# One-hot selection and the sum of output halves moved to GpSimd and DMA in a clustered attention and two-layer-pair kernel

## The chip, the cores and the metric

The kernel runs as one program on one core of a Trainium2 chip. The time is device microseconds of one execution. Lower is better. Five engines work side by side, each through its own instructions in order: TensorE (PE; PEld is its weight load), VectorE (DVE), ScalarE (ACT), GpSimd (POOL), and SyncE (SP), which here issues every transfer. TensorE writes to PSUM; GpSimd works on SBUF alone.

## The reference

Inputs are float32: q, k, v of 2 x 8 x 768 x 64, centroids of 8 x 16 x 64, and the weights of two pairs of layers. First comes attention within clusters; each query and key belongs to the centroid with the greatest cosine, and pairs in different clusters are masked:

```python
q_assign = np.argmax(np.einsum('bhsd,hcd->bhsc', q_n, c_n), axis=-1)
k_assign = np.argmax(np.einsum('bhsd,hcd->bhsc', k_n, c_n), axis=-1)
mask = q_assign[:, :, :, None] == k_assign[:, :, None, :]
scores = scale * np.matmul(q, k.transpose(0, 1, 3, 2))
scores = np.where(mask, scores, -1000000000.0)
scores = scores - np.max(scores, axis=-1, keepdims=True)
attn = np.exp(scores)
attn = attn / (np.sum(attn, axis=-1, keepdims=True) + 1e-09)
attn_out = np.matmul(attn, v)
```

The result, 1536 tokens of 512, goes through `relu(x @ w_in)**2 @ w_out` (512 to 2048 to 512; the float64 weights are read as pairs of 32-bit words), and then through four experts of 512 to 1024 to 512 whose outputs are weighted with `domain_probs` and summed.

## The kernel before, in words

**Numbers.** Matrices are split in two: a rounded float32r "high" part and a "low" part, the difference. A product takes three matmuls in the two layer pairs. In attention the high and low parts are stacked: `vv` holds the high part of v in 64 columns and the low part in the other 64, so one matmul gives two halves of the output that must be added.

**Attention.** There are 16 heads of 6 query blocks of 128 (96 blocks, numbered g or u in the code). For a block, `emit_S` makes the scores (four matmuls of 384 columns, L479; the first two over q and k, the last two over a low part and, in 16 more rows, a one-hot code of the cluster that does the masking), `emit_max` the row maximum on VectorE (L488), `emit_exp` the exponential on ScalarE (L499), `emit_T` six transposes on TensorE (L512) with the rounding copy on ScalarE (L517, `pth`) and the difference on VectorE (L518, `ptl`), `emit_PV` the product with `vv` (L526, L528; 12 matmuls for two blocks). `emit_PO` (L533) takes the product of two blocks out of PSUM: ScalarE copies one half to `tmp` (L542), VectorE adds the other (L544) into `xs`.

**What prepares a head.** Pairs of heads are loaded together. Four transpose slots per pair (`trans_slot`) leave `kqf` by ScalarE; GpSimd rounds it by adding a broadcast tile of zeros (L361) and subtracts (L363) into `nkh`, `nkl`, `nqh`, `nql`. `stack` (L367) copies these by DMA into the stacked tiles k1, q0, q1, k2, q2. `assign_slot` multiplies with the centroids (12 matmuls, L384); `onehot_ops` (L396) finds the greatest cosine and turns it to a one-hot code in seven VectorE operations (L420 to L427), the last two writing `oh`; ties go to the first centroid by the weights `wgt`. Two `onehot_slot`s transpose the code by three tiles each (L440), ScalarE copies it to `ohm` (L445), and two transfers (L448) put it into rows 64 to 79 of q2 and k2.

**What ends a pair of heads.** `norm_slots` makes the reciprocal of the row sums (f1), transposes it (f2), spreads it over rows with matmuls and multiplies (f3, L584), rounds (L596) and subtracts (L598) on GpSimd into `xh` and `xl`, the input of the layers.

**What sets the order.** Engines run in the order in which the code issues. `ORDER` (L24) lists the steps of an even and of an odd block: S, M and E are scores, maximum and exponential of later blocks, T, H and L the transposes and their two exits, P0 and P1 the product, O its exit, X1 and X2 two places for a slot and Y1, Y2 for its exit, R loads, stacks and the split of v, C one operation of the one-hot chain from the list `dq`, K one step of weight conversion from the list `cq` (even blocks from the eighth on). `AT` (L30) says how many blocks before a head its slots come, `START` (L28) where they come for the first heads. A one-hot slot first issues all that is left in `dq`. ScalarE's and GpSimd's instructions are issued at the slot's exit, so GpSimd's queue holds, in this order for an odd head, the split of v, four splits of k and q, and for an even head the exit of f3.

**Weights.** The first chunk of `w_in` is converted from float64 words during attention (`split64`, five VectorE operations on `cva` for each of four blocks, L153 to L165, issued as three and then two at one K, then a rounding and a subtraction); two loads of 1 MB of `w_out` follow in the same list. The rest is loaded and converted during the layers (`run_plan`), where TensorE works through 144 blocks of `gemm1` (L618 to L620) and `gemm2` (L648).

Of the kernel before, what the change touches and what calls it, by code (L numbers as in the profile page):

```python
# [34 lines left out]
def moe_attention_kernel(  # L35
# [15 lines left out]
    def eng(x):  # L51
        return {"V": nc.vector, "P": nc.gpsimd}[FL[x]]

# [43 lines left out]
    w_t = {}  # L97

# [36 lines left out]
    def split64(ci, part, j, cv):  # L135
# [13 lines left out]
        def f1():  # L149


            a = st["a"] = cv.tile(shp, F32, tag="cva", name="cva")
            nc.vector.tensor_scalar(  # L153
                a.bitcast(I32), high, 0x7FFFFFFF, None, op0=ALU.bitwise_and)
            nc.vector.tensor_scalar(a, a, 2.0 ** -15, None, op0=ALU.max)
            nc.vector.tensor_scalar(
                a.bitcast(I32), a.bitcast(I32), 3, 0x3FFFFFF8,
                op0=ALU.logical_shift_left, op1=ALU.bitwise_and)

        def f2():  # L160
            ai = st["a"].bitcast(I32)
            nc.vector.scalar_tensor_tensor(  # L162
                out=ai, in0=high, scalar=-0x40000000, in1=ai,
                op0=ALU.bitwise_and, op1=ALU.bitwise_or)
            nc.vector.scalar_tensor_tensor(  # L165
                out=ai, in0=low, scalar=29, in1=ai,
                op0=ALU.logical_shift_right, op1=ALU.bitwise_or)
# [6 lines left out]
        return [[f1, f2], [f3]]  # L174
# [23 lines left out]
    with tc.manual_schedule():  # L198
# [77 lines left out]
        vt, stk, kq, ohs, ohm = {}, {}, {}, {}, {}  # L276
        dq = []

        def split_v(i):
# [4 lines left out]
            if FL["vh"] == "A":  # L284
                nc.scalar.copy(hi, a)
            else:
                nc.gpsimd.tensor_tensor(hi, a, zeros.to_broadcast([128, NTT, D]), op=ALU.add)
            eng("vl").tensor_tensor(
                vv[:, :, D - vo:2 * D - vo], a, hi.bitcast(F32), op=ALU.subtract)

        def double(i, nm):
# [3 lines left out]
            for e in range(2):  # L295
                if i == 0:
                    nc.vector.tensor_copy(t[:, :, e], x)
                else:
                    nc.gpsimd.tensor_tensor(
                        t[:, :, e], x, zeros.to_broadcast([128, NTT, D]), op=ALU.add)  # L300
# [9 lines left out]
        def split_direct(i, nm, m):  # L310
# [14 lines left out]
            if nm == "nk":  # L325
# [6 lines left out]
                        lambda: nc.gpsimd.tensor_tensor(  # L332
                            second[top], both[top].bitcast(F32),
                            zeros[top].to_broadcast([D, 2, HALF]), op=ALU.add))
# [6 lines left out]
        def trans_slot(j, nm, half):  # L341

            def f():
# [52 lines left out]
        def onehot_ops(i, A):  # L396
# [7 lines left out]
            def p1():  # L404
                nc.gpsimd.tensor_tensor(A, A, mx.to_broadcast(shp), op=ALU.subtract)
                nc.gpsimd.tensor_scalar(A, A, 0.0, None, op0=ALU.is_ge)
                nc.gpsimd.tensor_tensor(A, A, wgt.to_broadcast(shp), op=ALU.mult)

            def p2():
                nc.gpsimd.tensor_tensor(A, A, mx2.to_broadcast(shp), op=ALU.subtract)  # L410
                nc.gpsimd.tensor_scalar(
# [547 lines left out]
```

## Time and profile before

| | |
|---|---|
| three runs | 1105.01, 1106.34, 1107.47 us; median 1106.34 |
| the profiled execution | 1102.88 us, its span 1100.8 us |
| TensorE (PE) busy | 1066.0 us, 97% of the span |
| VectorE (DVE) busy | 546.6 us, 50% |
| ScalarE (ACT) busy | 441.5 us, 40% |
| GpSimd (POOL) busy | 297.1 us, 27% |
| mean granted clock of TensorE | 0.992 |

The span runs from the first to the last instruction; what lies around it is the difference to the execution's time. Busy is the union of an engine's instructions. Attention fills the first 305 us or so, the layers the rest. In rows in order of time, the first number is the start in us from the span's start, the second the duration, "xN" says that N instructions of one kind stand in the row, and a bracket at the end gives idle time of the engine before it and what ended it. In rows of groups, what stands behind the bar is the group's busy us, the mean ns of one, and the idle us before them.

### The profile page before, as it was taken

What the parts mean: (1) busy time and instruction counts of PE and PEld (TensorE: products, weight loads), DVE (VectorE), ACT (ScalarE), POOL (GpSimd) and SP (SyncE); (2) the same over time, 40 slices, a digit from 0 to 9 for tenths busy, and PEclk for the clock granted to TensorE, in tenths of its full rate; (3) what the DMA queues carried; (4) which work ended last, traced back from release to release, by engine and by line L of the source; (5) the groups of instructions that cost most, each with busy time, mean ns of one, the idle gap of its engine ahead of it and who ended that gap; (6) DMA issues with size and microseconds to landing.
All of it is one profiled execution on the core that took longest, in us unless ns stands there. A gap on an engine that the chain in (4) does not pass through costs nothing.

```text
span 1100.8 us, 14190 instructions
## 1 busy us (share of the span) xinstructions
PE 1066.0 (97%) x5502; PEld 903.7 (82%) x5502; DVE 546.6 (50%) x950; ACT 441.5 (40%) x894; POOL 297.1 (27%) x300
## 2 busy tenths in 40 slices
PE   7887989999999999999999999999999999999998
PEld 7786879898877888888888888888888888888886
DVE  8799979999978884741012322222222223222322
ACT  6576778888855553434432121111212112121110
POOL 3346436544212222224544021110202112020000
PEclk9899999999999999999999999999999999999999
DMA  5564385645112331220111111020111101000012
GB/s 150 131 149 110 81 229 118 143 113 114 27 34 84 112 115 39 77 77 0 41 37 39 39 39 39 1 77 1 39 39 39 39 1 45 32 1 1 1 39 76
DMA packets 51810, 70.60 MB, mean 64 GB/s; under 512 B 25664, under 2 KB 28224, under 8 KB 51744
## 3 DMA queue, kind: packets, MB, share of 16 engines
q1 hardware_dynamic: 51744, 69.70, 22.9%
q8 instruction: 43, 0.70, 0.3%
q14 instruction: 23, 0.19, 0.1%
HBM read 43.05 MB, written 3.15 MB: 42 GB/s over the span
## 4 chain that ended last, share of the span: by engine, by line
PE 84%; DVE 11%; ACT 2%; DMA 1%; issue 1%; POOL 1%; SPq 0%; POOLq 0%; DVEq 0%
PE o L648 34%; PE h L620 11%; PE h L618 11%; PE h L619 11%; PE t L512 4%; PE s L479 4%; DVE ptl L518 2%; PE po L526 2%; PE po L528 2%; PE m L384 1%; DVE nb L488 1%; DVE cva L162 1%; DVE cva L165 1%; DMA k<-nkh 1%; PE m L577 1%
## 5 line engine op out<-in xcount | busy, mean ns | idle before, releaser
L632 DVE SCALAR_TENSOR_TENSOR hl<-h,hh 128x512 fp32r<-128x512 f32 x96 | 66.4, 692 | 393.4 <-ACT hh L631 393.4
L631 ACT ACTIVATE hh<-h 128x512 fp32r<-128x512 f32 x96 | 57.4, 598 | 429.0 <-PE h L620 429.0
L618 PE MATMUL h<-xh,w0h 128*128 128x512 f32 x560 | 217.8, 389 | 0.0
L619 PE MATMUL h<-xl,w0h 128*128 128x512 f32 x560 | 217.8, 389 | 0.0
L620 PE MATMUL h<-xh,w0l 128*128 128x512 f32 x560 | 217.8, 389 | 0.0
L648 PE MATMUL o<-w1h,hh 128*128 128x512 f32 x384 | 149.4, 389 | 0.0
L648 PE MATMUL o<-w1l,hh 128*128 128x512 f32 x384 | 149.4, 389 | 0.0
L648 PE MATMUL o<-w1h,hl 128*128 128x512 f32 x384 | 149.4, 389 | 0.0
L618 PEld LDWEIGHTS h<-xh,w0h 128*128 128x128 f32 x560 | 105.3, 188 | 21.8
L620 PEld LDWEIGHTS h<-xh,w0l 128*128 128x128 f32 x560 | 105.1, 188 | 21.9
L619 PEld LDWEIGHTS h<-xl,w0h 128*128 128x128 f32 x560 | 105.1, 188 | 21.7
L629 POOL TENSOR_TENSOR hl<-r,hh 128x512 fp32r<-128x512 f32 x48 | 63.1, 1314 | 184.3 <-ACT hh L628 127.5
L518 DVE TENSOR_TENSOR ptl<-t,pth 128x384 fp32r<-128x384 f32 x192 | 100.2, 548 | 14.9 <-ACT pth L517 13.9
L183 POOL TENSOR_TENSOR w0l<-raw,w0h 128x512 fp32r<-128x512 f32 x32 | 41.3, 1291 | 236.7 <-ACT w0h L182 236.7
L512 PE MATMUL t<-identf,p 128*128 128x128 f32 x576 | 93.3, 287 | 12.2 <-DVE ptl L518 11.2
L488 DVE TENSOR_REDUCE nb<-s 128x1 f32<-128x768 f32 x96 | 90.9, 947 | 10.2 <-PE s L479 9.5
L517 ACT CAST pth<-t 128x384 fp32r<-128x384 f32 x192 | 84.4, 479 | 28.4 <-PE t L512 26.4
L499 ACT ACTIVATE p<-s,nb 128x768 f32<-128x768 f32 x96 | 86.8, 904 | 10.3 <-DVE nb L488 9.7
L479 PE MATMUL s<-k,q 80*128 80x384 f32 (+1 forms) x384 | 88.7, 354 | 0.2 <-DVE q L321 0.2
L512 PEld LDWEIGHTS t<-identf,p 128*128 128x128 f32 x576 | 65.6, 144 | 27.1 <-DVE ptl L518 24.2
L648 PEld LDWEIGHTS o<-w1l,hh 128*128 128x128 f32 x384 | 72.1, 188 | 15.0
L648 PEld LDWEIGHTS o<-w1h,hl 128*128 128x128 f32 x384 | 72.1, 188 | 15.0
(142 smaller groups left out, 1662.3 us busy)
## 6 DMA issues: line engine op xcount, KB each, us to landing
raw<-in_moe_w_dram SPq DMA_DIRECT2D x16, 1024.0 KB, 5.1
raw<-in_moe_w_in_dram SPq DMA_DIRECT2D x8, 1024.0 KB, 5.3
raw<-in_moe_w_out_dram SPq DMA_DIRECT2D x8, 1024.0 KB, 4.9
q<-nqh SPq DMA_DIRECT2D x42, 192.0 KB, 3.0
k<-nkh SPq DMA_DIRECT2D x28, 192.0 KB, 3.9
q<-nql SPq DMA_DIRECT2D x28, 192.0 KB, 3.8
nv<-in_v_dram SPq DMA_DIRECT2D x16, 192.0 KB, 4.3
out_dram<-acc SPq DMA_DIRECT2D x12, 256.0 KB, 2.1
```

The costliest lines, as they stand in the source:

```text
L479: nc.tensor.matmul(s[:, j, 0:HALF], stk[i, nq][:, t * 128:(t + 1) * 128], stk[i, nk][:, j * HALF:(j + 1) * HALF], start=first, stop=not first)
L488: nc.vector.tensor_reduce(out=nb, in_=s_ps[u][:, :, 0:HALF], axis=AX.XY, op=ALU.max, negate=True)
L499: nc.scalar.activation(p, s_ps.pop(u)[:, :, 0:HALF], AF.Exp, bias=nb_t.pop(u), accum_out=sums_t[hp][:, i % 2, t:t + 1])
L512: nc.tensor.transpose(tp[:, j], p_sb[u][:, half, j * 128:(j + 1) * 128], identf)
L517: return (lambda: nc.scalar.copy(dh, tp), lambda: nc.vector.tensor_tensor(dl, tp, dh.bitcast(F32), op=ALU.subtract))
L518: lambda: nc.vector.tensor_tensor(dl, tp, dh.bitcast(F32), op=ALU.subtract))
L618: nc.tensor.matmul(ps, wh[:, kt, ms], xh[tb][:, kt], start=(kt == 0), stop=False)
L619: nc.tensor.matmul(ps, wh[:, kt, ms], xl[tb][:, kt], start=False, stop=False)
L620: nc.tensor.matmul(ps, wl[:, kt, ms], xh[tb][:, kt], start=False, stop=(kt == KD - 1))
L629: nc.gpsimd.tensor_tensor(hl, r, hh.bitcast(F32), op=ALU.subtract)
L632: nc.vector.scalar_tensor_tensor(out=hl, in0=ps, scalar=0.0, in1=hh.bitcast(F32), op0=ALU.max, op1=ALU.subtract)
L648: nc.tensor.matmul(o_t[n], a, b, start=(ft == 0 and z == 0), stop=(ft == NF - 1 and z == 2))
```

## The change

From the third head on, the one-hot chain between the two maxima runs on GpSimd: three operations behind the first maximum (a subtraction, a multiplication by 2^126 in two steps, an addition), four list places left empty, the second maximum on VectorE, then four operations. The comparisons become arithmetic with minimum and maximum, and the query's code is 0 and -1 where it was 1 and 0. Heads 0 and 1 keep VectorE's chain. The one-hot code is transposed two tiles at a time, in one slot a head in place of two, and goes to q2 and k2 in four transfers in place of two.

`emit_PO` copies the whole product (128 partitions) by ScalarE into `xs` or `xo`; when a head is done, transfers move the halves so that high and low parts lie in the same partitions of `xs` and `xm`, and one GpSimd addition per pair of heads (at f2's exit) sums them. The last pair keeps the addition on VectorE.

GpSimd's rounding copies multiply by 1.0 twice (`round_pool`) in place of adding zeros. `kqf` has three buffers in place of two. The five VectorE steps of `split64` are issued one at each K, and the two 1 MB loads of `w_out` become eight of 256 KB, each in a K of its own; the list is 32 entries long in place of 14.

```diff
-START = {'t': [1, 3, 3, 3], 'stack1': 6, 'stack': 7, 'head': [[1, 2, 3], [7, 8, 8]]}
-FL = {"chain": "V", "po": "V", "xh": "P", "xm": "P", "xl": "P", "kh": "P", "kl": "P", "vh": "P", "vl": "P"}
-AT = {"gap": 3, "stack1": -11, "stack": -9, "assign": -9, "oh0": -5, "oh1": -4, "splitv": -3,
+START = {'t': [1, 3, 3, 3], 'stack1': 6, 'stack': 7, 'head': [[1, 2], [7, 8]]}
+AT = {"gap": 4, "stack1": -11, "stack": -9, "assign": -9, "oh": -4, "splitv": -3,
       "t0": -15, "t1": -14, "t2": -13, "t3": -13, "conv": 8}
...
+    def round_pool(dst, src):
+
+        nc.gpsimd.tensor_scalar(dst, src, 1.0, 1.0, op0=ALU.mult, op1=ALU.mult)
...
+    def load_piece(half, n):
+
+        if n == 0:
+            raw_t[0, 1, half] = rawp.tile([128, 2048], F32, tag="raw", name="raw")
+        r = raw_t[0, 1, half].bitcast(I32).rearrange("p (k f) -> p k f", k=2)
+        kk, fs = n // 2, slice((n % 2) * 512, (n % 2) * 512 + 512)
+        nc.sync.dma_start(out=r[:, kk, fs], in_=wo32[:, half * 2 + kk, fs])
...
         def f1():
-
-
             a = st["a"] = cv.tile(shp, F32, tag="cva", name="cva")
+            st["i"] = a.bitcast(I32)
+            nc.vector.tensor_scalar(st["i"], high, 0x7FFFFFFF, None, op0=ALU.bitwise_and)
+
+        def f2():
+            nc.vector.tensor_scalar(st["a"], st["a"], 2.0 ** -15, None, op0=ALU.max)
+
+        def f4():
             nc.vector.tensor_scalar(
-                a.bitcast(I32), high, 0x7FFFFFFF, None, op0=ALU.bitwise_and)
-            nc.vector.tensor_scalar(a, a, 2.0 ** -15, None, op0=ALU.max)
-            nc.vector.tensor_scalar(
...
-        def f2():
-            ai = st["a"].bitcast(I32)
+        def f5():
             nc.vector.scalar_tensor_tensor(
-                out=ai, in0=high, scalar=-0x40000000, in1=ai,
+                out=st["i"], in0=high, scalar=-0x40000000, in1=st["i"],
                 op0=ALU.bitwise_and, op1=ALU.bitwise_or)
+
...
-        return [[f1, f2], [f3]]
+        return [[f1, f2, f4, f5, f6], [f3]]
...
-            if FL["vh"] == "A":
-                nc.scalar.copy(hi, a)
-            else:
-                nc.gpsimd.tensor_tensor(hi, a, zeros.to_broadcast([128, NTT, D]), op=ALU.add)
-            eng("vl").tensor_tensor(
+            round_pool(hi, a)
+            nc.gpsimd.tensor_tensor(
                 vv[:, :, D - vo:2 * D - vo], a, hi.bitcast(F32), op=ALU.subtract)
 
...
-                    x = kq_p.tile([128, HALF], F32, tag="kqf", name="kqf", bufs=2)
+                    x = kq_p.tile([128, HALF], F32, tag="kqf", name="kqf", bufs=3)
                     nc.scalar.activation(x, m, AF.Copy, scale=mul)
-                    if FL["kh"] == "A":
-                        nc.scalar.copy(hi, x)
-                    else:
-                        nc.gpsimd.tensor_tensor(
-                            hi, x, zeros[:, 0].to_broadcast([128, HALF]), op=ALU.add)
-                    eng("kl").tensor_tensor(lo, x, hi.bitcast(F32), op=ALU.subtract)
+                    round_pool(hi, x)
+                    nc.gpsimd.tensor_tensor(lo, x, hi.bitcast(F32), op=ALU.subtract)
...
+            if i > 1:
+
+                P = nc.gpsimd
+
+                def p1():
+                    P.tensor_tensor(A, A, mx.to_broadcast(shp), op=ALU.subtract)
+                    P.tensor_scalar(A, A, 2.0 ** 63, 2.0 ** 63, op0=ALU.mult, op1=ALU.mult)
+                    P.tensor_tensor(A, A, wgt.to_broadcast(shp), op=ALU.add)
+
+                def p2():
+                    P.tensor_tensor(A, A, mx2.to_broadcast(shp), op=ALU.subtract)
+                    P.tensor_scalar(oh[:, :, 0], A[:, NTT:2 * NTT], 0.0, -1.0,
+                                    op0=ALU.min, op1=ALU.max)
+                    P.tensor_scalar(off, A[:, 0:NTT], 0.0, -1.0, op0=ALU.min, op1=ALU.max)
+                    P.tensor_scalar(oh[:, :, 1], off, 1.0, -NEG, op0=ALU.add, op1=ALU.mult)
+
                 return [lambda: V.reduce_max(out=mx, in_=A, axis=AX.X), p1] + [
                     lambda: None] * AT["gap"] + [
                     lambda: V.reduce_max(out=mx2, in_=A, axis=AX.X), p2]
...
+        def onehot_slot(i):
...
+                om = as_p.tile([4 * C, HALF], F32R, tag="ohm", name="ohm")
+                m = ps_m.tile([4 * C, HALF], F32R, tag="m", name="m")
+                for a in range(QT):
                     nc.tensor.transpose(
-                        m[:, t * 128:(t + 1) * 128],
-                        ohs[i][:, half * QT + t].rearrange("p s c -> p (s c)"), identr)
+                        m[:, a * 128:(a + 1) * 128],
+                        ohs[i][:, 2 * a:2 * a + 2].rearrange("p t s c -> p (t s c)"), identr)
 
                 def evac():
-                    nc.scalar.copy(ohm[i][:, half * HALF:(half + 1) * HALF], m.bitcast(F32))
-                    if half == 1:
-                        for nm, r in (("q2", 0), ("k2", C)):
+                    nc.scalar.copy(om, m.bitcast(F32))
+                    for s, nm in enumerate(("q2", "k2")):
+                        for e in range(2):
+                            r = (2 * e + s) * C
                             nc.sync.dma_start(
-                                out=stk[i, nm][D:D + C].bitcast(F32),
-                                in_=ohm[i][r:r + C].bitcast(F32))
+                                out=stk[i, nm][D:D + C].bitcast(F32).rearrange(
+                                    "c (a e n) -> c a e n", a=QT, e=2)[:, :, e],
+                                in_=om[r:r + C].bitcast(F32).rearrange("c (a n) -> c a n", a=QT))
...
-        def emit_PO(pr, last=False):
...
+            po = po_t.pop(pr)
+            cs = slice(jj * 256, (jj + 1) * 256)
+            if e == 0 and jj == 0:
                 xs_t[hp] = xs_p.tile([128, S], F32, tag="xs", name="xs")
-            po = po_t.pop(pr)
-            a, z = D * (i % 2), D * (1 - i % 2)
-            tmp = xs_p.tile([128, 256], F32, tag="tmp", name="tmp")
-            xs = xs_t[hp][a:a + D, jj * 256:(jj + 1) * 256]
-            nc.scalar.copy(tmp[a:a + D], po[z:z + D])
-            if last or FL["po"] == "V":
-                nc.vector.tensor_tensor(xs, po[a:a + D], tmp[a:a + D], op=ALU.add)
-            else:
-                nc.scalar.copy(xs, po[a:a + D])
-                nc.gpsimd.tensor_tensor(xs, xs, tmp[a:a + D], op=ALU.add)
+            if hp == NH // 2 - 1:
+                a, z = D * e, D * (1 - e)
+                tmp = xs_p.tile([128, 256], F32, tag="tmp", name="tmp", bufs=1)
+                nc.scalar.copy(tmp[a:a + D], po[z:z + D])
+                nc.vector.tensor_tensor(xs_t[hp][a:a + D, cs], po[a:a + D], tmp[a:a + D], op=ALU.add)
+                return
+            if e == 1 and jj == 0:
+                xo_t[hp] = xs_p.tile([128, S], F32, tag="xo", name="xo", bufs=1)
+            nc.scalar.copy((xo_t if e else xs_t)[hp][:, cs], po)
+            if jj == NTT // 2 - 1:
+                top, low = slice(0, D), slice(D, 2 * D)
+                if e == 0:
+                    xm_t[hp] = xs_p.tile([128, S], F32, tag="xm", name="xm", bufs=1)
+                    nc.sync.dma_start(out=xm_t[hp][top], in_=xs_t[hp][low])
+                else:
+                    xo = xo_t.pop(hp)
+                    nc.sync.dma_start(out=xs_t[hp][low], in_=xo[low])
+                    nc.sync.dma_start(out=xm_t[hp][low], in_=xo[top])
...
                 def evac():
                     rt = st["rt"] = xs_p.tile([NTT * 4, 128], F32R, tag="rt", name="rt")
                     nc.scalar.copy(rt, m.bitcast(F32))
+                    if hp in xm_t:
+                        xm = xm_t.pop(hp)
+                        nc.gpsimd.tensor_tensor(xs_t[hp], xs_t[hp], xm, op=ALU.add)
                 return evac
...
-                        if last or FL["xh"] == "A":
+                        if last:
                             nc.scalar.copy(hi, xn)
                         else:
-                            nc.gpsimd.tensor_tensor(
-                                hi, xn, zeros[:, 0].to_broadcast([128, n]), op=ALU.add)
-                        (nc.vector if last else eng("xl")).tensor_tensor(
+                            round_pool(hi, xn)
+                        (nc.vector if last else nc.gpsimd).tensor_tensor(
...
+            for n, x in enumerate(("assign", "oh")):
                 at(slots, START["head"][i - 1][n] if i < 3 else u0 + AT[x],
-                   onehot_slot(i, n - 1) if n else assign_slot(i))
+                   onehot_slot(i) if n else assign_slot(i))
...
         cq = []
         for j in range(NF):
             cq += [f for fs in split64(0, 0, j, cv_p[0]) for f in fs]
-        for n, x in enumerate(w_loads(0)[2:]):
-            cq.append(lambda x=x: load_w(*x))
+        for half in range(2):
+            cq += [lambda half=half, n=n: load_piece(half, n) for n in range(4)]
```

## Rows read from the trace of the kernel before

**Rows 1.** Stretch, length, busy us (instructions) of PE, PEld, DVE, ACT, POOL; clock, DMA, GB/s

```profile
58.70:176.80 118.10, 103.63 (x744) 93.74 (x743) 105.30 (x204) 86.27 (x201) 57.90 (x64) 0.96 0.56 133
176.80:276.50 99.70, 97.77 (x741) 89.11 (x739) 93.86 (x186) 83.26 (x197) 50.75 (x60) 1.00 0.56 130
...
346.00:1094.00 748.00, 745.81 (x3291) 617.46 (x3290) 240.56 (x357) 190.57 (x330) 151.16 (x117) 1.00 0.12 40
```

**Rows 2.** The row maxima (L488) alone, heads 8 to 13

```profile
176.80:276.50 99.70, 33.97 (x36) 1.00 0.56 130
```

**Rows 3.** VectorE in order of time, head 11: start us, duration, instruction

```profile
226.31 0.94 DVE L488 TENSOR_REDUCE nb<-s 128x1 f32<-128x768 f32 x1
227.17 0.34 DVE L421 TENSOR_TENSOR A<-A,mx 128x192 f32<-128x192 f32 x1
227.44 1.01 DVE L518 TENSOR_TENSOR ptl<-t,pth 128x384 fp32r<-128x384 f32 x2
...
228.64 0.94 DVE L488 TENSOR_REDUCE nb<-s 128x1 f32<-128x768 f32 x1
```

**Rows 4.** TensorE in order of time, heads 13 and 14

```profile
271.32 0.86 PE L479 MATMUL s<-k,q 128*128 128x384 f32 x4
...
274.70 0.88 PE L479 MATMUL s<-k,q 128*128 128x384 f32 x4
...
282.27 0.87 PE L479 MATMUL s<-k,q 128*128 128x384 f32 x4
282.97 0.34 PE L440 MATMUL m<-identr,oh 128*32 128x128 f32 x3
283.15 0.88 PE L512 MATMUL t<-identf,p 128*128 128x128 f32 x6
...
284.58 0.86 PE L479 MATMUL s<-k,q 128*128 128x384 f32 x4
```

**Rows 5.** VectorE's writers of `oh` (length, busy, count); L544 (count, busy, mean ns)

```profile
58.70:290.00 231.30, 15.22 (x26) 0.98 0.53 126
...
L544 DVE TENSOR_TENSOR xs<-po,tmp 64x256 f32<-64x256 f32 x48 | 20.1, 419 | 2.0 <-ACT tmp L542 1.3
```

**Rows 6.** One operation's duration ns: min, median, max

```profile
L426 DVE TENSOR_SCALAR oh<-off x16: 189/204/1054, 15.6 to 279.6; 128x96 fp32r<-128x96 f32 x16
```

**Rows 7.** Groups of instructions on GpSimd: xcount, busy us, mean ns

```profile
L629 POOL TENSOR_TENSOR hl<-r,hh 128x512 fp32r<-128x512 f32 x48 | 63.1, 1314 | 184.3 <-ACT hh L628 127.5 <-issue 28.6 <-PE o L648 28.1
...
L584 POOL TENSOR_TENSOR rb<-rb,xs 128x384 f32<-128x384 f32 x14 | 14.2, 1014 | 81.0 <-ACT rb L583 81.0
...
L361 POOL TENSOR_TENSOR nkh<-kqf,zeros 128x384 fp32r<-128x384 f32 x14 | 11.8, 839 | 41.3 <-DMA k<-nkh 19.6 <-ACT kqf L357 19.2 <-ACT p L499 2.4
...
masks.py:199 POOL TENSOR_SCALAR_AFFINE_SELECT identf<-identf 128x128 f32<-128x128 f32 x1 | 0.3, 294 | 0.1
```

**Rows 8.** Instructions on `cva` in attention: length, busy of DVE, ACT, POOL

```profile
6.00:300.00 294.00, 13.38 (x20) 2.53 (x4) 5.11 (x4) 0.97 0.52 125
```

**Rows 9.** All engines in order of time, the stall in head 6

```profile
139.15 1.06 SPq L110 DMA_DIRECT2D raw<-in_moe_w_out_dram  x1
...
144.13 0.83 POOL L361 TENSOR_TENSOR nkh<-kqf,zeros 128x384 fp32r<-128x384 f32 x1 [6.74 <-DMA k<-nkh]
...
146.60 0.90 PE L350 MATMUL m<-identf,nq 128*128 128x128 f32 x3 [4.13 <-ACT kqf L357]
```

**Rows 10.** One-hot transfer on SP, its time to landing, and the matmuls that read it

```profile
238.36 0.59 SPq L448 DMA_DIRECT2D k<-ohm  x1
...
DMA to landing us min/median/max: 2.1/2.1/2.2
...
241.75 0.95 PE L479 MATMUL s<-k,q 128*128 128x384 f32 x4
```

**Rows 11.** Fourth split on GpSimd, and the one-hot transposes behind it

```profile
217.07 1.02 POOL L363 TENSOR_TENSOR nql<-kqf,nqh 128x384 fp32r<-128x384 f32 x1
...
220.32 0.42 PE L440 MATMUL m<-identr,oh 128*32 128x128 f32 x3
```

More of the change, by code (lines that the diff above doesn't have):

```diff
@@ L152, in f1, with f6 @@
             a = st["a"] = cv.tile(shp, F32, tag="cva", name="cva")
+            st["i"] = a.bitcast(I32)
[3 more added lines that the diff above has]
+        def f4():
             nc.vector.tensor_scalar(
[L154 to L157 removed]
+                st["i"], st["i"], 3, 0x3FFFFFF8,
                 op0=ALU.logical_shift_left, op1=ALU.bitwise_and)
[L160 to L161 removed]
+        def f5():
             nc.vector.scalar_tensor_tensor(
[L163 removed]
+                out=st["i"], in0=high, scalar=-0x40000000, in1=st["i"],
                 op0=ALU.bitwise_and, op1=ALU.bitwise_or)
+        def f6():
             nc.vector.scalar_tensor_tensor(
[L166 removed]
+                out=st["i"], in0=low, scalar=29, in1=st["i"],
                 op0=ALU.logical_shift_right, op1=ALU.bitwise_or)
@@ L269, in moe_attention_kernel @@
                 idv[:, :, h, 1:2].to_broadcast([NTT * 4, NTT, D]), op=ALU.add)
-        vt, stk, kq, ohs, ohm = {}, {}, {}, {}, {}
+        vt, stk, kq, ohs = {}, {}, {}, {}
         dq = []
@@ L298, in double @@
                 else:
-                    nc.gpsimd.tensor_tensor(
-                        t[:, :, e], x, zeros.to_broadcast([128, NTT, D]), op=ALU.add)
+                    round_pool(t[:, :, e], x)
         def trans_direct(i, nm):
@@ L331, in split_direct @@
                 return (lambda: lo(both[low], low, hi),
-                        lambda: nc.gpsimd.tensor_tensor(
-                            second[top], both[top].bitcast(F32),
-                            zeros[top].to_broadcast([D, 2, HALF]), op=ALU.add))
+                        lambda: round_pool(second[top], both[top].bitcast(F32)))
             else:
@@ L402, in onehot_ops @@
             V = nc.vector
[L404 to L411, printed above, removed]
-                    oh[:, :, 1], A[:, 0:NTT], 0.0, NEG, op0=ALU.is_lt, op1=ALU.mult)
-                nc.gpsimd.tensor_scalar(oh[:, :, 0], A[:, NTT:2 * NTT], 0.0, None, op0=ALU.is_ge)
-            if FL["chain"] == "P" and i > 0:
+            if i > 1:
[10 more added lines that the diff above has]
+                    P.tensor_scalar(oh[:, :, 1], off, 1.0, -NEG, op0=ALU.add, op1=ALU.mult)
                 return [lambda: V.reduce_max(out=mx, in_=A, axis=AX.X), p1] + [
@@ L430, in onehot_ops @@
             ]
-        def onehot_slot(i, half):
+        def onehot_slot(i):
             def f():
@@ L467, in pair_slots @@
             return [trans_slot(j, nm, half) for nm in ("nk", "nq") for half in range(2)]
-        s_ps, p_sb, nb_t, sums_t, pt_t, po_t, xs_t = {}, {}, {}, {}, {}, {}, {}
+        s_ps, p_sb, nb_t, sums_t, pt_t, po_t, xs_t, xo_t, xm_t = {}, {}, {}, {}, {}, {}, {}, {}, {}
         def emit_S(u):
@@ L583, in evac @@
                     nc.scalar.copy(rb, m)
-                    (nc.vector if last else eng("xm")).tensor_tensor(
+                    (nc.vector if last else nc.gpsimd).tensor_tensor(
                         rb, rb, xs_t[hp][:, half * HALF:(half + 1) * HALF], op=ALU.mult)
@@ L592, in evac @@
                         hi = xh[tb][:, kt, o:o + n]
-                        if last or FL["xh"] == "A":
+                        if last:
                             nc.scalar.copy(hi, xn)
                         else:
-                            nc.gpsimd.tensor_tensor(
-                                hi, xn, zeros[:, 0].to_broadcast([128, n]), op=ALU.add)
-                        (nc.vector if last else eng("xl")).tensor_tensor(
+                            round_pool(hi, xn)
+                        (nc.vector if last else nc.gpsimd).tensor_tensor(
                             xl[tb][:, kt, o:o + n], xn, hi.bitcast(F32), op=ALU.subtract)
@@ L799, in moe_attention_kernel @@
                     at(early, START[x] if i == 2 else u0 + AT[x], lambda i=i, n=n: stack(i, n))
-            for n, x in enumerate(("assign", "oh0", "oh1")):
+            for n, x in enumerate(("assign", "oh")):
                 at(slots, START["head"][i - 1][n] if i < 3 else u0 + AT[x],
-                   onehot_slot(i, n - 1) if n else assign_slot(i))
+                   onehot_slot(i) if n else assign_slot(i))
             at(early, u0 + AT["splitv"], lambda i=i: split_v(i))
@@ L893, in moe_attention_kernel @@
         emit_PV(pr, 1)
-        emit_PO(pr, True)
+        emit_PO(pr)
         whole(f3)
```

10 lines of the change are left out of this document (2 added, 8 removed).

## The prediction

> **What bounds the kernel now.** I read the page first, then busy times by stretch, then two engines in order of time. Behind 346 us TensorE is busy for 745.8 of 748 us and VectorE for a third of it [rows 1]; the change touches nothing there, so only attention can move. There a head is six query blocks, each with one row maximum (L488) on VectorE. Heads 8 to 13 are 36 of these in 99.7 us [rows 1, 2], so 2.77 us a block, 16.62 a head. TensorE shows 97.8 us busy there and VectorE 93.9; ScalarE (83.3) and GpSimd (50.8) have room. The two high numbers don't mean the same. TensorE's rows overlap (four score matmuls are written as 0.87 us and the next group starts 0.70 after them [rows 4]), so its union hides short waits. VectorE in order of time has none to hide: from one maximum to the next, 228.64 - 226.31 = 2.33 us, stand the maximum, two `ptl` subtractions and two operations of the one-hot chain at about 0.27 from start to start, no idle mark before any [rows 3]. Without these two it would be 1.8.
>
> What TensorE needs I take from starts, where little is waited for. A block with one one-hot slot takes 284.58 - 282.27 = 2.31, the slot 283.15 - 282.97 = 0.18 of it, so 2.13 without; a block with an assign slot takes 274.70 - 271.32 = 3.38, so the slot costs 1.25 for 12 matmuls, 0.10 each [rows 4]. The head after the change: 6 x 2.13 + 1.25 + 0.18 + about 9.5 small matmuls (transposes of k and q, normalisation) at 0.10 = 15.2 us. Against 16.62 VectorE sets the pace by a small margin.
>
> Heads 2 to 7, as many blocks, take 118.1 us, and VectorE is busy for 105.3 of it [rows 1]. The same work is there, plus 13.4 us of weight conversion on VectorE (20 operations on `cva` [rows 8]) and one stall: a stack transfer lands late next to a 1 MB weight load, GpSimd waits 6.74 us, TensorE 4.13 [rows 9]. The clock granted over this stretch is 0.96, over heads 8 to 13 it is 1.00 [rows 1].
>
> **The change, part by part.** *VectorE, chain.* The two operations that write `oh` are 15.22 us in 13 heads, 1.17 each [rows 5]; the three before them are about 0.34 each [rows 3]. Together 2.2 us a head. *VectorE, halves.* Three additions (L544) a head at 0.419 go, 1.26 [rows 5]; ScalarE's copy stays, with twice the partitions. VectorE falls from 93.86/6 = 15.6 to 12.2 a head, well under TensorE's 15.2; ScalarE is at 83.26/6 = 13.9 [rows 1]. So TensorE is late next.
>
> *GpSimd.* A two-input operation is 1.01 us at 384 and 1.31 at 512 columns [rows 7], so 0.56 at 192 and 1.91 at 768. No row shows a one-input `tensor_scalar` there. From below it isn't cheaper than the 0.29 us of the 128-column select with three times the columns, from above hardly dearer than the two-stream 1.01; the copy with broadcast zeros takes 0.84 [rows 7]. The nearest row is the select (one read, one write), 0.88 if all of it scaled with columns. I take 0.6 at 384, which with the select's 0.29 makes 0.37 at 192 and 0.26 at 96. First part of the chain: 0.56 + 0.37 + 0.56 = 1.5; second: 0.56 + 3 x 0.26 = 1.3. GpSimd's head: 8.5 now [rows 1], + 2.8, + 1.9/2 for the added sum, - 4 x 0.24 for roundings = 11.3 of 15.6. It has the throughput; the question is what waits for it.
>
> The Trainium skill (GPSIMD Engine Reference, section 4.1 Engine selection) speaks against the move: elementwise work belongs on VectorE, GpSimd being about twice as slow with two inputs and roughly at line rate with one. By its line rate at 1.2 GHz a 384-column rounding would be an estimated 0.4 us with a start, and the sum below would be near 1075.
>
> *New waits.* The second maximum on VectorE waits for GpSimd's first part, two blocks after it was issued: hidden; behind it would stand L488 and L518, and TensorE behind those. The one-hot transposes now wait for the second part on GpSimd. For odd heads it is queued behind four k/q splits: these now end at 217.07 + 1.02 = 218.1, the transposes start at 220.32 [rows 11], 2.2 us later. Of this go 1.2 (the one-hot transfers are four instead of two, 0.59 each on SP [rows 10], and the k/q stack transfers that release the splits are queued behind them on SP), 1.2 (five blocks, each 0.23 shorter), 1.3 (second part itself); four cheaper roundings give 1.0 back: 0.5 us late. And the last one-hot transfer, issued at 238.36, lands 2.1 later at 240.5 and is read at 241.75 + 0.35 (half of 0.70): 1.6 spare, of which go 1.2 and two shorter blocks, 0.5: about nothing left. I take 0.4 us a head for both, between 0 and 1.0. The three SP transfers of halves are issued four blocks ahead of the addition that reads them and cost nothing; late, they would hold GpSimd's queue.
>
> *Packed transposes.* One slot of 0.18 goes each head (in the 15.2). *Weight conversion in single steps.* The 13.4 us stay but spread over some eight heads instead of four, VectorE then at 12.2 + 1.7 a head; I charge a third, 4.5 us, for maxima held up behind a step, between 0 and all 13.4. *Load in pieces* of 256 KB, well after that stall: it goes. *Start, and heads 14 and 15*: counted at nothing; a third `kqf` buffer may gain, the flush of head 2's chain may lose, so -4 to +2.
>
> **Sum.** Heads 8 to 13: 99.7 - 6 x (15.2 + 0.4) = -6.1. Heads 2 to 7: 118.1 - 93.6 - 4.5 = -20.0. The profiled execution took 1102.9 us (span 1100.8, 2.1 around it); less 26.1 it is 1076.8. The median of the runs, 1106.3, is 3.5 above that execution: 1080.
>
> **Rivals.** *TensorE is already the bound* in heads 8 to 13. For it: 97.8 of 99.7 busy. Against it: VectorE without a gap [rows 3]. Then a head there only loses its slot, 16.4 us: -1.3, and heads 2 to 7 come to 98.4 + 4.5: -15.2. Time 1090.
>
> *The shared port.* The same 96-column operation L426 takes 189 ns at least and 1054 at most [rows 6]; I read the long ones as waits for a GpSimd instruction. With GpSimd busier, the 20 conversion steps may each take up to 0.85 more: 17 us, VectorE at 12.2 + 30.4/8 = 16.0 a head for eight heads, 0.8 over TensorE: +6. Time 1086. The Trainium skill (Advanced Engine Details and Errata, section GPSIMD Details) has GpSimd share a read and a write interface with VectorE, in conflict with its 2-port modes and with two SBUF inputs; the trace agrees, 189 against 1054 ns.
>
> *One input is no cheaper than two.* Per pair of heads, five roundings and six short operations stand ahead of the transposes, 6.5 times the price above 0.6. At 0.95: 2.3 a pair, 14 over six pairs. Time 1094.
>
> *Slower: GpSimd becomes the engine that everybody waits for*, at the one-hot transposes. It eats the gain from 26.1/39 = 0.67 above 0.6, so from 1.27 us for a 384-column one-input operation with two operations in it. At 1.6 it is +39: 1119. Against it: both priced two-input rows are cheaper. For it: no row shows the operation.
>
> *The pieces don't help*: eight transfers fall where stack transfers run again, and the 4.1 us and the clock dip behind it come back: 1085.
>
> **Chances.** Forecast 0.48, its own range 1067 to 1092 (waits 0 to 1.0 a head, conversion 0 to 9, start); TensorE-bound 0.15; port 0.12; dear one-input 0.12; slower 0.10; pieces 0.03. From 1065 to 1100 all but the slower case and an edge is held. A measurement tells about 0.2%, 2.2 us, from no change. Only the slower rival ends above 1108.5; near its break-even lies the 0.03 for no change: faster 0.87, slower 0.10.
>
> **What would show it.** Right: L544 gone but for the last pair, block spacing near 2.6 us in heads 2 to 13, VectorE below 85% busy there, GpSimd near 70%, no wait of several us on `nkh`, a rounding between 0.4 and 0.8 us. Wrong: TensorE's one-hot transposes waiting for GpSimd by more than 1 us a head, `mx` operations on VectorE waiting for GpSimd, score matmuls waiting for a one-hot transfer, roundings at 0.95 us or more.

## The result and the profile after

The changed kernel takes 1088.19 us (median of 4 runs, 1085.11 to 1090.40), the kernel before, beside it, 1105.99: a ratio of 0.9836, 95% interval 0.9803 to 0.9869. The forecast was 1080 with a range of 1065 to 1100: faster, as said, by some 18 us instead of 26. The profiled execution took 1090.28 us, its span 1088.5 at a mean granted clock of 0.990. In the runs further down, one execution of e10's kernel (3723.21 us) and one of the kernel before beside it (1191.29 us) were far longer than the rest; the ratios leave them out, and without them the two medians given there, 1072.85 and 1105.88, are 1072.10 and 1105.6.

Taken from the starts of the first row maximum of heads 2, 8 and 14 (58.77, 176.81, 276.54 before; 53.09, 156.50, 261.45 after) and the two spans:

| stretch | forecast | measured |
|---|---|---|
| start to head 2 | 0 | -5.7 |
| heads 2 to 7 | -20.0 | -14.6 |
| heads 8 to 13 | -6.1 | +5.2 |
| head 14 to the end | 0 | +2.8 |
| sum | -26.1 | -12.3 |

The two profiled executions lie 12.6 us apart, the medians 17.8. About 3 us of the difference stand in head 3 of the changed kernel's execution, which ran at a granted clock of 0.83 (e2 below has this head without it), so the row of heads 2 to 7 shows that much too little gain.

Stretches of the changed kernel: length, then busy us (instructions) of PE, PEld, DVE, ACT, POOL, granted clock, DMA share, GB/s.

```profile
53.10:156.50 103.40, 97.23 (x725) 90.81 (x724) 87.94 (x154) 81.31 (x193) 68.34 (x106) 0.97 0.64 150
156.50:261.40 104.90, 97.66 (x722) 91.16 (x721) 80.37 (x142) 80.08 (x190) 67.46 (x109) 0.97 0.66 159
...
345.00:1088.00 743.00, 739.61 (x3264) 612.08 (x3262) 228.71 (x345) 181.93 (x314) 148.48 (x115) 1.00 0.12 39
```

Against [rows 1], VectorE is down to 80.37 of 104.90 us (77%) in heads 8 to 13, and GpSimd up from 50.75 to 67.46; still the stretch is longer. Heads 8 to 13 now hold one head of 21.74 us, head 10:

```profile
190.10:211.90 21.80, 18.72 (x123) 17.30 (x122) 13.00 (x25) 14.01 (x33) 11.34 (x21) 0.86 0.85 214
```

The DMA engines are busy for 0.85 of it, and the granted clock over it is 0.86. The chain of waits through head 10 (start, us, what):

```profile
197.25 1.01 POOL nql L366
198.26 0.06 POOL nqh L52
198.32 7.03 DMA k<-nkl
205.35 0.14 issue
205.49 0.98 PE m L387 x6
```

and what SP issued around it:

```profile
196.67 0.94 SPq L105 DMA_DIRECT2D raw<-in_moe_w_out_dram  x1
197.71 0.51 SPq L378 DMA_DIRECT2D k<-nkh  x1
198.32 0.54 SPq L380 DMA_DIRECT2D k<-nkl  x1
...
201.08 0.55 SPq L566 DMA_DIRECT2D xs<-xo  x1
201.68 0.60 SPq L567 DMA_DIRECT2D xm<-xo  x1
```

A stack transfer needs 7.03 us beside a piece of `w_out` and two transfers of halves; the stall that head 6 had [rows 9] stands in head 10.

Heads 3, 5, 7 and 9 are late at another place. VectorE, then GpSimd, at the start of head 9:

```profile
172.90 0.95 DVE L497 TENSOR_REDUCE nb<-s 128x1 f32<-128x768 f32 x1
173.82 1.02 DVE L527 TENSOR_TENSOR ptl<-t,pth 128x384 fp32r<-128x384 f32 x2
174.76 2.29 DVE L178 SCALAR_TENSOR_TENSOR cva<-raw,cva 128x512 int32<-128x512 int32 x1
176.97 0.94 DVE L497 TENSOR_REDUCE nb<-s 128x1 f32<-128x768 f32 x1
```

```profile
174.66 1.84 POOL L593 TENSOR_TENSOR xs<-xs,xm 128x768 f32<-128x768 f32 x1
```

The block, from one maximum to the next, takes 4.07 us; in it one conversion step, L178, takes 2.29. The step starts 0.10 behind the GpSimd sum of the halves and ends 0.55 behind that sum's end. All four L178 of heads 2 to 9 meet a sum (instruction, count, min/median/max ns):

```profile
L178 DVE SCALAR_TENSOR_TENSOR cva<-raw,cva x4: 1989/2278/2285, 70.9 to 174.8; 128x512 int32<-128x512 int32 x4
```

Prices on GpSimd between 50 and 262 us, which is heads 2 to 13 and a little beside them (count, busy us, mean ns, idle before); they answer to [rows 7]:

```profile
L593 POOL TENSOR_TENSOR xs<-xs,xm 128x768 f32<-128x768 f32 x6 | 11.0, 1836 | 0.0
L414 POOL TENSOR_TENSOR A<-A,wgt 128x192 f32<-128x192 f32 x13 | 7.8, 597 | 1.1
...
L412 POOL TENSOR_TENSOR A<-A,mx 128x192 f32<-128x192 f32 x13 | 6.7, 513 | 34.0 <-DVE mx L423 34.0
L52 POOL TENSOR_SCALAR nkh<-kqf 128x384 fp32r<-128x384 f32 x12 | 6.4, 536 | 10.3 <-DMA k<-nkh 8.7 <-ACT kqf L364 1.6
...
L413 POOL TENSOR_SCALAR A<-A 128x192 f32<-128x192 f32 x13 | 4.6, 354 | 1.1
...
L418 POOL TENSOR_SCALAR oh<-A 128x96 fp32r<-128x96 f32 x12 | 3.2, 268 | 1.1
```

Waits of TensorE in heads 2 to 13 (us in total, times, longest):

```profile
PE m L447 <- POOL oh L421: 5.8, 8, 1.0
PE t L521 <- DVE ptl L527: 5.1, 4, 1.4
PE m L387 <- DMA k<-nkl: 2.1, 1, 2.1
```

5.8/12 = 0.5 us a head is the wait of the one-hot transposes for GpSimd, which the forecast had between 0 and 1.0. Over these heads a block takes 2.89 us on average (208.36 us for 72), where 2.6 was the sign of a right forecast.

### The profile page after: what moved, and what is told of

Read it like the earlier page. It is cut to its first block, busy times and chain, and to the rows that moved or that the text cites. A ratio compares the mean times of both kernels' runs of the same rounds, so it can differ in the third digit from the quotient of the medians.

```text
span 1088.5 us, 14186 instructions
## 1 busy us (share of the span) xinstructions
PE 1058.7 (97%) x5457; PEld 903.1 (83%) x5457; DVE 504.3 (46%) x838; ACT 431.9 (40%) x879; POOL 326.2 (30%) x405
## 4 chain that ended last, share of the span: by engine, by line
PE 75%; DVE 3%; POOL 2%; DMA 2%; ACT 1%; issue 1%; SPq 0%; POOLq 0%; ACTq 0%
PE o L670 35%; PE h L642 11%; PE h L640 11%; PE h L641 11%; PE t L521 2%; PE s L488 1%; PE po L535 1%; PE po L537 1%; DVE cva L173 1%; PE m L387 1%; DMA k<-nkh 1%; DMA k<-nkl 1%; DVE cva L178 0%; PE m L600 0%; POOL nql L366 0%
## 5 line engine op out<-in xcount | busy, mean ns | idle before, releaser
L497 DVE TENSOR_REDUCE nb<-s 128x1 f32<-128x768 f32 x96 | 91.2, 950 | 15.3 <-PE s L488 14.6
L521 PE MATMUL t<-identf,p 128*128 128x128 f32 x576 | 89.6, 284 | 5.7 <-DVE ptl L527 5.6
L488 PE MATMUL s<-k,q 80*128 80x384 f32 (+1 forms) x384 | 87.7, 350 | 2.1 <-DMA k<-ohm 1.8
L670 PEld LDWEIGHTS o<-w1h,hh 128*128 128x128 f32 x384 | 72.0, 188 | 15.0
```

The lines of the kernel that those rows point to most:

```text
L488: nc.tensor.matmul(s[:, j, 0:HALF], stk[i, nq][:, t * 128:(t + 1) * 128], stk[i, nk][:, j * HALF:(j + 1) * HALF], start=first, stop=not first)
L497: nc.vector.tensor_reduce(out=nb, in_=s_ps[u][:, :, 0:HALF], axis=AX.XY, op=ALU.max, negate=True)
L521: nc.tensor.transpose(tp[:, j], p_sb[u][:, half, j * 128:(j + 1) * 128], identf)
L670: nc.tensor.matmul(o_t[n], a, b, start=(ft == 0 and z == 0), stop=(ft == NF - 1 and z == 2))
```

## The experiments

Each group of four was timed beside the kernel before (medians 1106.34 for e1 to e4, 1104.59 for e5 to e8, 1105.88 for e9 to e12); between groups the ratio is what compares.

**e1, fewer empty places in the chain**

```diff
-AT = {"gap": 4, ...
+AT = {"gap": 2, ...
```

> The second part of the one-hot chain is issued two list places earlier, ahead of f3's exit for even heads and ahead of the fourth k/q split for odd heads; nothing else changes. Theory (the relief of VectorE is eaten by TensorE's one-hot transposes, which wait for GpSimd's second part): heads 8 to 13 lose most of the about 0.8 us a head of that wait, so do heads 2 to 7; 8 to 11 us off the changed kernel, about 1079 us. Rival (TensorE's own work is the bound and the wait only moves to the next group): 1086 to 1089 us.

Measured 1087.9 us, ratio 0.9828 (0.9809 to 0.9846). The wait at L447 is gone, and a new one stands at the assign slot:

```profile
PE m L387 <- DMA q<-nql: 7.1, 6, 1.4
```

The rival's range. That the one-hot wait is what the change lost falls: behind it the last stack transfer is as late.

**e2, the pieces of `w_out` from block 80 on**

```diff
-    "K": lambda: g >= AT["conv"] and cq and cq.pop(0)(),
+    "K": lambda: (g >= 80 or len(cq) > 8 and g >= AT["conv"]) and cq and cq.pop(0)(),
```

> The eight 256 KB loads move from blocks 56 to 70 to blocks 80 to 94, where few stack transfers are left; nothing else changes. Theory (the 8.2 us block at the end of head 10 is a stack transfer that lands late beside the pieces): that block falls to about 3.5 us and the dip of the granted clock behind it goes, 4 to 7 us off where the stall shows, about 1083 us. Rival (the transfers of the halves and of the one-hot code delay the stack transfers): the stall stays or appears in another head, 1086 to 1090 us.

Measured 1082.9 us, 0.9782 (0.9767 to 0.9797): head 10 falls from 21.74 to 18.17 us. Head 3 falls as well, from 20.27 to 17.28, but no piece was loaded there: its granted clock was 0.83 in the changed kernel's execution, and this one has 1.00 over all of heads 2 to 7, where it was 0.97. Heads 2 to 7 and 8 to 13:

```profile
53.00:153.50 100.50, 94.09 (x725) 87.94 (x724) 87.34 (x153) 80.94 (x193) 68.54 (x106) 1.00 0.67 154
153.50:254.20 100.70, 95.38 (x722) 89.54 (x720) 80.36 (x142) 80.31 (x190) 67.71 (x110) 0.98 0.63 145
```

**e3, the chain back on VectorE**

```diff
-            if i > 1:
+            if i > NH:
```

> The one-hot chain runs on VectorE for all heads as before the change; halves, packed transposes, rounding, pieces and third kqf buffer stay. Theory (VectorE at 14.4 us a head is already below TensorE's 15.4, and without the chain on GpSimd no transposes wait for it): as fast as the changed kernel or faster, 1082 to 1089 us, no wait of the transposes for GpSimd. Rival (moving the chain is what made the gain): 1094 us or more.

Measured 1084.87 us, 0.9793 (0.9773 to 0.9812). Net, the chain's move earns nothing in the changed kernel. But this run takes away more than the chain: without it GpSimd comes to the sum of the halves earlier (the first at 67.9 us, the first step L178 at 72.7; in the changed kernel 70.8 and 70.9), and the step meets no sum any more:

```profile
L178 DVE SCALAR_TENSOR_TENSOR cva<-raw,cva x4: 679/682/689, 72.7 to 173.4; 128x512 int32<-128x512 int32 x4
```

So two effects stand against each other here, VectorE's extra work and the meeting that is gone, and the run doesn't tell what the chain's move is worth by itself.

**e4, the halves back on VectorE** (`emit_PO` and the sum as before the change)

> The output halves are added on VectorE straight from PSUM as before the change; chain on GpSimd, packed transposes, rounding, pieces and third kqf buffer stay. Theory: VectorE is back by 1.26 us a head to 13.5, below TensorE's 15.4; GpSimd loses 0.9 us a head and SP three transfers a pair, so stack transfers land earlier: 1084 to 1090 us, with a smaller stall in head 10. Rival (each us of VectorE counts): 1 us a head over 14 heads dearer, about 1102 us.

Measured 1079.47 us, 0.9750 (0.9735 to 0.9766), below the range expected. The move of the halves cost 8.7 us. The step L178, without the sum on GpSimd:

```profile
L178 DVE SCALAR_TENSOR_TENSOR cva<-raw,cva x4: 670/670/675, 72.9 to 169.5; 128x512 int32<-128x512 int32 x4
```

And head 10, with the pieces of `w_out` where the changed kernel has them, but no transfers of halves:

```profile
183.20:200.90 17.70, 16.55 (x128) 15.22 (x126) 14.20 (x30) 13.86 (x32) 10.34 (x18) 1.00 0.81 204
```

It takes 17.54 us at a clock of 1.00, 4.2 less than in the changed kernel: the pieces alone do not make the whole stall.

**e5, a second buffer for `nkh`** (`bufs=2` for that tile alone)

> The kernel after with one change: the tile nkh (rounded key rows of one half) has two buffers instead of one; 3 KB more per partition, no instruction added or removed. Theory: heads 2 to 13 are paced by a chain that is handed on once per pair of heads: stack transfer k<-nkh lands, only then may GpSimd write the next nkh, then three more key/query splits follow on GpSimd, then the next stack transfers, and TensorE's assign slot waits for the last of these. The larger number of SP transfers after the change made its first link longer. With a second buffer GpSimd no longer waits for that landing (3.3 us in odd heads), so the splits end 2 to 3 us earlier in each pair and the stall of 8 us in head 10 shrinks: 1076 to 1083 us. Rival A: the waiting of GpSimd was free, since what TensorE waits for is the last stack transfer q<-nql on SP or the PE work of 15.4 us a head itself: 1086 to 1089 us, and the even heads stay above 16.4 us. Rival B: the splits then run beside other GpSimd and VectorE work at a worse moment: above 1090 us.

Measured 1085.78 us, 0.9822 (0.9788 to 0.9856), which can't be told from the changed kernel. GpSimd no longer waits for `k<-nkh`, but in head 10 the last stack transfer, `q<-nql`, lands as late as `k<-nkl` did:

```profile
201.47 5.97 DMA q<-nql
207.45 0.14 issue
207.58 1.43 PE m L388 x6
```

So this hand-over is not what loses the time by itself.

**e6, single conversion steps and late pieces alone, on the kernel before**

```diff
-        return [[f1, f2], [f3]]
+        return [[f1, f2, f4, f5, f6], [f3]]
...
-        for n, x in enumerate(w_loads(0)[2:]):
-            cq.append(lambda x=x: load_w(*x))
+        for half in range(2):
+            cq += [lambda half=half, n=n: load_piece(half, n) for n in range(4)]
```

> The kernel before with one part of the change alone: weight conversion in single VectorE steps, and w_out of the first expert in eight pieces of 256 KB, issued from block 80 on. Chain, halves, transposes and roundings are as before. Theory: the stall of 6.7 us on GpSimd and 4.1 us on TensorE beside the 1 MB load in head 6, and the bursts of conversion in heads 3 to 7, go; heads 2 to 7 then come near the 16.6 us of heads 8 to 13: 118.1 falls to 102 to 106, so the time is 1091 to 1096 us, and this part alone is most of what the whole change gained. Rival: the conversion steps cost VectorE the same 13.4 us in whatever order, and only the stall goes: 1099 to 1103 us.

Measured 1089.51 us, 0.9843 (0.9804 to 0.9882). Heads 2 to 7 and 8 to 13:

```profile
63.20:166.70 103.50, 99.99 (x751) 90.61 (x751) 98.81 (x202) 84.10 (x201) 55.22 (x63) 1.00 0.56 130
166.70:267.00 100.30, 97.91 (x740) 88.89 (x739) 94.95 (x190) 83.22 (x196) 52.02 (x61) 1.00 0.55 129
```

VectorE is busy for 98.81 us there against 105.30 [rows 1]. This part alone gains 15.1 us, a little more than expected and nearly what the whole change does; its pieces come late, as in e2, not where the change has them.

**e7, one-input roundings and the third `kqf` alone, on the kernel before**

```diff
-                nc.gpsimd.tensor_tensor(hi, a, zeros.to_broadcast([128, NTT, D]), op=ALU.add)
+                round_pool(hi, a)
```

> The kernel before with one part of the change alone: the roundings on GpSimd read one input (384 columns in 0.51 to 0.56 us instead of 0.84) and kqf has three buffers instead of two. Theory: the 5 us that the start and head 0 lost in the change (first maximum 18.74 to 17.28, head 0 19.21 to 15.72) come from these, since GpSimd's key and query splits are all that the first heads wait for; in heads 8 to 13 VectorE still paces, unchanged at 16.6 us: 1100 to 1103 us. Rival: the early gain comes from the chain or the halves that left VectorE: 1105 to 1107 us here.

Measured 1094.29 us, 0.9892 (0.9862 to 0.9922): 10.3 us, more than expected.

```profile
56.30:169.80 113.50, 103.08 (x743) 93.51 (x742) 102.08 (x204) 85.87 (x201) 49.94 (x64) 0.95 0.58 139
169.80:267.00 97.20, 97.09 (x742) 89.40 (x741) 91.32 (x187) 82.80 (x197) 43.22 (x60) 1.00 0.57 133
```

The first maximum starts at 17.17 us (18.74 before), as in the theory. But heads 8 to 13 fall too, and only the even ones: 15.3 to 15.4 us instead of 16.2, the odd ones stay at 17.05. In the even heads the second block took 3.71 us and now takes 2.7. In it stands an operation of the one-hot chain that writes `oh`. Head 10 of the kernel before, GpSimd and VectorE:

```profile
213.32 1.01 POOL L363 TENSOR_TENSOR nkl<-kqf,nkh 128x384 fp32r<-128x384 f32 x1
213.35 1.05 DVE L426 TENSOR_SCALAR oh<-off 128x96 fp32r<-128x96 f32 x1
```

and of this run:

```profile
204.83 1.02 POOL L362 TENSOR_TENSOR nkl<-kqf,nkh 128x384 fp32r<-128x384 f32 x1
205.64 0.27 DVE L425 TENSOR_SCALAR oh<-off 128x96 fp32r<-128x96 f32 x1
```

Before, the operation starts 0.03 us behind a GpSimd subtraction, takes 1.05 us and ends 0.07 behind the subtraction's end; here GpSimd's splits run earlier, the subtraction is nearly over, and it takes 0.27. Heads 8 and 12 show the same. This is the meeting of the conversion step and the sum once more, at another pair of instructions. In the odd heads, of which [rows 3] show one, the other writer of `oh` takes 0.93 us in both kernels, beside GpSimd's multiplication at f3's exit, where it takes 0.24 in the even heads here. So VectorE was without a gap, but in neither kind of head was all of its time its own work. Whether the cheaper rounding or the third `kqf` gave the gain was not tried apart.

**e8, halves on VectorE, late pieces, two `nkh`** (e2, e4 and e5 together)

> The kernel after with three changes: the halves of the output are added on VectorE again (as before the change), the eight pieces of w_out are issued from block 80 on, and nkh has two buffers. Theory: halves on VectorE alone gave 1079.5, late pieces alone took 5.3 us off; head 10 then no longer stalls in either, so the two gains overlap in part (2 to 3 us remain), and the second nkh buffer takes 2 to 6 us more: 1070 to 1076 us. Rival: the same stall is met by all three and nothing adds: 1078 to 1081 us.

Measured 1074.87 us, 0.9718 (0.9689 to 0.9748). No head stalls: odd heads 15.5 to 15.8 us, even ones 16.5 up to head 8, then 15.9 and 15.6.

**e9, e2 with no conversion step beside the sum of the halves**

```diff
-(g >= 80 or len(cq) > 8 and g >= AT["conv"])
+(g >= 80 or len(cq) > 8 and g >= AT["conv"] and g % 12 not in (4,))
```

> The kernel with late pieces (1082.9 us, its pieces of w_out issued from block 80 on) with one change: no weight conversion step is issued in the block in which the second head of a pair begins (the fifth of each twelve, counted at issue), so the steps use five blocks in twelve instead of six. Theory: the sum of the halves on GpSimd (768 columns with two inputs, 1.84 us) holds up the VectorE step that is issued with it: the step L178 takes 2.27 us in the changed kernel, 0.67 us where the halves are added on VectorE, four times of four; with the step elsewhere the odd heads 3, 5, 7 and 9 fall from 17.3 to about 15.7, 6.4 us in all, less up to 3 us for steps that now meet GpSimd's key and query splits: 1076.5 to 1080 us. Rival: it was the addition's own time or the transfers of the halves that held the odd heads, not the meeting of the two: 1082 to 1085 us, and the first gap of odd heads stays near 4.0 us.

Measured 1076.72 us, 0.9736 (0.9712 to 0.9760).

```profile
L178 DVE SCALAR_TENSOR_TENSOR cva<-raw,cva x4: 682/863/1011, 78.1 to 192.0; 128x512 int32<-128x512 int32 x4
```

The sum and its transfers stand as before; only the meeting is gone, and the first gap of the odd heads is 2.08 us and less where it was 4.0. Against e2 the time is 6.2 us lower by medians, 5.1 by the ratios.

**e10, e8 with no conversion step beside the key and query splits** (`g % 12 not in (10,)`)

> The kernel with halves on VectorE, late pieces and two nkh buffers (1074.9 us) with one change: no conversion step is issued in the block in which the first head of a pair begins, where GpSimd does the key and query splits. Theory: there the step L165 takes 1.12 us instead of 0.42 and the block 3.6 us instead of 2.55 (four times), so the heads 2, 4, 6 and 8 fall from 16.5 to about 15.8: 1071 to 1073 us. Rival: another step that now falls beside GpSimd's work costs as much, or TensorE sets the pace of these heads with its extra transposes: 1074 to 1076 us.

Measured 1072.85 us, 0.9704 (0.9676 to 0.9732), as expected, the lowest time here and 33 us under the kernel before. Its interval overlaps that of e8.

```profile
54.60:149.30 94.70, 93.97 (x727) 88.58 (x726) 88.54 (x169) 81.81 (x192) 63.30 (x104) 1.00 0.61 142
149.30:244.10 94.80, 94.21 (x723) 87.85 (x722) 85.96 (x162) 81.40 (x191) 63.05 (x105) 1.00 0.58 136
```

**e11, e8 with the chain back on VectorE** (`if i > NH:`)

> The kernel with halves on VectorE, late pieces and two nkh buffers (1074.9 us) with one change: the one-hot chain of every head runs on VectorE, as before the change. Theory: the chain is 2.2 us a head of VectorE and VectorE then paces again: odd heads back to 17.05 us, as with the roundings alone, even heads 15.4 to 16.5; over heads 2 to 13 about 6 x 1.4 us more: 1081 to 1085 us. Rival: with halves moved by DMA, taking the chain back gained 3 us, so the move of the chain is worth nothing or less: 1072 to 1076 us.

Measured 1086.92 us, 0.9829 (0.9806 to 0.9852): 12 us slower than e8, a little more than expected.

```profile
56.40:160.00 103.60, 98.29 (x735) 89.04 (x733) 101.23 (x202) 83.84 (x197) 48.97 (x65) 1.00 0.57 132
160.00:258.50 98.50, 95.35 (x714) 86.44 (x713) 94.84 (x190) 80.79 (x188) 42.91 (x59) 1.00 0.55 130
```

VectorE is busy for 98% and 96% of the two stretches: here it does set the pace. Part of that is held-up time again: the two writers of `oh` take 14.37 us over heads 2 to 13 (24 operations), where they take 6.15 in e3.

**e12, halves by DMA and on GpSimd, with everything else of e10** (`g % 12 not in (4, 10)`)

> The changed kernel (halves moved by DMA and added on GpSimd) with late pieces, two nkh buffers, and no conversion step in the blocks in which a head of a pair begins (both of the above). Theory: what the move of the halves cost, 8.7 us, was the meeting of its sum with the conversion steps (6.4 us) and the load of its transfers next to the stack transfers; with both taken away it costs nothing more: 1070 to 1074 us, the same as the kernel with halves on VectorE and the same spacing. Rival A: its three transfers of 196 KB a pair still delay the stack transfers: 1076 to 1080 us. Rival B: VectorE's relief of 1.26 us a head pays at last: under 1070 us.

Measured 1075.69 us, 0.9723 (0.9702 to 0.9744), between the theory and rival A; its interval overlaps e10's.

```profile
55.10:150.60 95.50, 93.30 (x725) 88.57 (x724) 81.11 (x148) 80.37 (x192) 67.31 (x105) 1.00 0.69 159
150.60:246.20 95.60, 93.71 (x723) 88.10 (x722) 81.85 (x148) 80.68 (x191) 69.23 (x109) 1.00 0.66 154
```

VectorE has 7.4 and 4.1 us less to do than in e10, and the stretches are no shorter. TensorE is busy for 98 to 99% of them in both, so it is most likely what is left to set the pace; no run took work from TensorE to show it.

## Why the forecast was right in sign and 8 us too low

**Right.** The prices: a rounding at 384 columns 0.51 to 0.57 us (0.6 taken), the chain 0.51 + 0.35 + 0.60 and 0.51 + 3 x 0.27 = 2.8 us a head (2.8 taken), the sum 1.84 (1.9). The pace: 15.2 + 0.4 us a head is close to what can be kept; e10 needs 94.7 and 94.8 us for six heads, 15.8 each, e12 15.9. The chain on VectorE costs 12 us when the other waits are gone (e8 against e11). With the roundings cheap, the rivals of a dear one-input operation and of a GpSimd that makes the kernel slower fall; with 15.8 us a head kept, so does the rival of TensorE bound at 16.4.

That 1088 lies within the range is in part luck: the start, counted at nothing, gave 5.7 us, while heads 8 to 13, where 6.1 were to be gained, lost 5.2.

**The step that failed** is "the three SP transfers of halves ... cost nothing", with the sum that hangs on them, which was counted only in GpSimd's own time. Moving the halves cost 8.7 us (e4 against the changed kernel). Most of that is one mechanism: the sum of 1.84 us is issued in the block in which the conversion step L178 runs, in heads 3, 5, 7 and 9, and the step takes 2.28 us instead of 0.67: 4 x 1.6 = 6.4. e9 issued the steps in other blocks and changed nothing else, and 5 to 6 us came back. The rest stands in head 10, below. The forecast had this mechanism as a rival, but with up to 0.85 us on each of 20 steps for 17 us in all; it hit four steps and cost twice that each, because the GpSimd instruction that it meets is the long one, which the change itself brought. The Trainium skill (Advanced Engine Details and Errata, section GPSIMD Details) names VectorE instructions with two SBUF inputs as one kind that conflicts; L178 is one, and the trace agrees, 2278 against 670 ns.

**"The stall goes"** also failed. Pieces of 256 KB in heads 9 to 11 fall beside stack transfers, and TensorE waits and loses clock as it did in head 6: 5.3 us between the medians (e2), a rival that I gave 0.03 of the chance. The halves' transfers have a part in it: head 10 takes 21.74 us with both, 18.17 with the pieces moved (e2) and 17.54 without the transfers (e4).

**Heads 8 to 13** were read from one odd head. e7 shows that in the even heads VectorE was held up beside GpSimd's splits, at the operation whose 1054 ns the forecast read rightly as such a wait [rows 6] and then priced for the conversion steps alone. The 2.2 us a head that it counts for the chain hold this time: the two writers of `oh`, 1.17 us together on average, are 0.20 + 0.24 where they meet nothing. The cheaper roundings with the third `kqf` therefore gain where I counted nothing, 1.6 us to the first maximum and 0.9 in each even head, and parts that I had added up stand in each other's place: steps with late pieces alone gain 15.1, roundings alone 10.3, together already more than the whole change.

**The way from 1088 to 1073**, by ratio: late pieces 0.9836 to 0.9782, no step beside the sum 0.9736, two `nkh` and no step beside the splits 0.9723, halves back on VectorE 0.9704. The first two steps lie outside the intervals, the last two do not: what the move of the halves costs without the meeting and the stall, 2 us by the ratios, is not told from nothing. The packed transposes were not tried by themselves. The 2.8 us from head 14 on were not followed up; e10 needs 1069.6 - 244.2 = 825.4 us from there, the kernel before 824.3, the changed one 827.1.

## What to carry to other kernels

When work is moved to GpSimd, look up which VectorE instruction stands beside it in the list, not only whether GpSimd has time: here the other one lost up to nearly the length of the GpSimd instruction, and one empty place in the list gave it back (e9). The busy time of an engine holds such waits, so compare the shortest and the longest duration of one operation before taking it for work. Read the pace from every kind of stage in a period, since two heads of a pair can be held up at different places. When a run takes a part back, look whether it also moves a meeting, as e3 does. And before adding up what parts of a change remove, ask for each whether another part removes the same wait.

## What the runs showed of the hardware

- A VectorE step of 512 columns with two inputs, 0.67 us alone, took 1.99 to 2.29 us beside a GpSimd addition of 768 columns (1.84 us); in head 9 it ended 0.55 us after it.
- A one-input VectorE operation of 96 columns, 0.19 to 0.20 us alone, took 1.05 when it started 0.03 us behind a GpSimd subtraction of 384 columns (1.01 us).
- GpSimd's one-input operation with two arithmetic steps took 0.27 us at 96 columns, 0.35 at 192, 0.51 to 0.57 on average at 384, where a copy that adds broadcast zeros took 0.84 at 384.
- A stack transfer of 192 KB took 7.03 us to land beside a 256 KB load and the halves' transfers, in a stretch at 214 GB/s; the median of its kind in that kernel was 4.1.
